# K-v products ahead of the turns of q, and three turns of x moved from TensorE to DMA, in an attention and SwiGLU kernel

One core of a Trainium2 chip. The metric is the device time of one execution in microseconds (us), the median of several. Engines: PE is TensorE, PEld its weight loads, DVE VectorE, ACT ScalarE, POOL GpSimd, SP SyncE. A number such as L513 is a line of the kernel before the change; the change shifts lines only from L680 on, so the groups named here keep their line, but for the program's closing waits: L801 before, L815 after, L808 and L818 in two of the experiments.

## The reference

Linear attention with cosine weights over 8 batches of 8 heads, 576 positions and 64 columns, then a feed-forward block over the 4608 rows that come out.

```python
def phi(x, c, s):
    r = np.maximum(x, 0.0)
    return np.concatenate([r * c, r * s], axis=-1)
q_p, k_p = phi(q, cos_w, sin_w), phi(k, cos_w, sin_w)
kv  = np.einsum('bhsf,bhsd->bhfd', k_p, v)        # the "k-v products"
z   = np.sum(k_p, axis=2)
num = np.einsum('bhsf,bhfd->bhsd', q_p, kv)       # "tile products", L444 and L399
den = np.einsum('bhsf,bhf->bhs', q_p, z)[..., None] + 1e-06
x   = (num / den)                                  # to 4608 rows of 512
g, val = x @ w_gate, x @ w_val                     # 512 to 1536, L513
out = (g * (1.0 / (1.0 + np.exp(-g))) * val) @ w_out   # L549
```

## The kernel before

The rows are worked in 36 tiles of 128. Four tiles make a group: twelve gate and value columns (`ffn_fc`), then four times twelve output products (`ffn_out`). Between these, in slots, stand the pieces of attention for the tiles to come. Two inputs of a tile need a turn (transpose): q before the tile products, x before the gate. Each is done on PE with a copy out of PSUM (`banks` in the views), or by a DMA transpose from SP. Code counts batches from 0; the text calls `b = 1` batch two, `b = 3` batch four.

```python
def relu_slots(b, lo, hi):
    ...
    relu_op("dve", st["qp"][:, b, lo:hi].rearrange("p c j (i d) -> p c (j i) d", i=2),
            raws[b, "q"][:, :, lo:hi].rearrange("p g c d -> p c g d"))

def qturn_pe(b, j, lo, hi, eng):                    # 7 turns of q and one copy out of PSUM
    ps = take(1).bitcast(BF16).rearrange("p (c x) -> p c x", x=P)
    for c in range(lo, hi):
        nc.tensor.transpose(out=ps[:, c - lo], in_=st["qp"][:, b, c, j], identity=ident)
    copy_op(eng, qt_of(b)[:, :, j, lo:hi].rearrange("p e c s -> p c e s"), ...)

def kv_mm(b): ...                                   # 72 products, L285, into two PSUM banks
def kv_out(b, engs=("act", "dve"), js=slice(0, J)): ...   # bank 0 on ACT, bank 1 on DVE, 2 copies each
...
def x_turn(t, fast=False):
    if fast:
        x_turn_pe(t)                                # four transposes on PE, L485
        x_turned(t, "act")                          # copy of 128x512
    else:
        nc.sync.dma_start_transpose(out=xT_of(t), in_=st["x", t])
...
at("b11", q_(1, 0, 0), q_(1, 1, 0), lambda: kv_mm(1), lambda: kv_out(1))
at((0, 0), lambda: kv_free(1), a_(4, 0), a_(4, 1))  # tile 4, after four output products
...
for nm in ("q", "k", "v"):                          # load_behind: one after the other
    load(b, nm)
...
elif tg == 2:                                       # tiles 9, 10, 11
    at((10, 11, 12)[i - 1] + SLOTS, lambda t=t: a_tile2(t))
    at((12, 13, 14)[i - 1] + SLOTS, turn(t, True))
```

## Time and profile before

| | us |
|---|---|
| median of three runs (lowest, highest) | 325.91 (325.68, 326.50) |
| span of the profiled run | 324.0 |
| PE busy | 317.4 |
| PE's waits, four in all | 2.7 |

The prediction below shows the page, PE's waits and the chain around both places that the change touches. ScalarE and VectorE at the first place (timeline, kernel before; columns: start us, us, engine, line, operation, output and input, then in brackets the idle time before it and its releaser):

```profile
38.74 1.08 DVE L220 TENSOR_SCALAR r_q<-raw_q 128x1792 bf16<-128x1792 bf16 x1
...
40.47 1.71 ACT L333 COPY phit<-banks 128x896 bf16<-128x896 bf16 x2 [1.66 <-PE banks L274]
42.10 0.76 ACT L297 CAST kvd<-banks 64x260 bf16<-64x260 f32 x2
42.15 0.87 DVE L297 CAST kvd<-banks 64x260 bf16<-64x260 f32 x2 [1.07 <-PE banks L285]
```

The one ReLU of 1.08 us stands between PE and its next work. The k-v copies (L297) end at 43.02, just as PE, with four output products done in the meantime, comes to the tile products that read them.

Second, SP's own waits at the end of the program (waits of SP; waited for: us in total, times, longest). It closes by waiting for the last transfers of the result:

```profile
SPq L801 <- DMA out_dram<-ob: 1.3, 2, 0.8
```

### The profile page before, as it was taken

Reading aid. Unit: us, or ns where it says so; the run is one execution under the profiler, and the core shown is the slowest. Engines: PE = TensorE matmul, PEld = TensorE weight load, DVE = VectorE, ACT = ScalarE, POOL = GpSimd, SP = SyncE. Lnnn points to the kernel's source line nnn. Section 1 sums busy time; section 2 is a strip of 40 time slices with the busy share of each in tenths; the row PEclk is TensorE's granted clock in tenths of the full one; section 3 lists DMA queues with packets and bytes.
Section 4 is the critical chain, followed back from the end, with each engine's and each line's share of the span. In section 5 each row is a group of like instructions: output and inputs, shape, how many; then the busy total and the mean of one; then the engine's idle time right before and its main releaser. Section 6 shows DMA issues by size and latency. Waiting matters only on the chain.

```text
span 324.0 us, 6046 instructions
## 1 busy us (share of the span) xinstructions
PE 317.4 (98%) x2396; PEld 159.8 (49%) x2396; DVE 181.5 (56%) x362; ACT 132.2 (41%) x242; POOL 34.9 (11%) x59
## 2 busy tenths in 40 slices
PE   8899899999999999999999999999999999999995
PEld 4596455455445444544454445444554445444443
DVE  7873867786475647565657555755564236423420
ACT  7453455653553335332632354344432132213311
POOL 6845002002000200020002000200000000000000
PEclk9999999999999999999999999999999999999999
DMA  7999998999675997699778969697921411240014
GB/s 274 211 200 197 206 190 119 219 119 156 146 121 80 162 184 122 91 140 145 172 106 114 172 149 129 87 170 158 135 45 35 104 26 34 40 104 19 0 32 99
DMA packets 72748, 40.64 MB, mean 125 GB/s; under 512 B 48272, under 2 KB 67472, under 8 KB 72720
## 3 DMA queue, kind: packets, MB, share of 16 engines
q1 hardware_dynamic: 50368, 22.55, 38.3%
q0 software_dynamic: 22192, 17.57, 37.4%
q8 instruction: 19, 0.31, 0.4%
q10 hardware_dynamic: 160, 0.13, 0.1%
q14 instruction: 9, 0.07, 0.1%
HBM read 37.75 MB, written 9.44 MB: 146 GB/s over the span
## 4 chain that ended last, share of the span: by engine, by line
PE 93%; DVE 4%; ACT 1%; issue 0%; ACTq 0%
PE banks L513 57%; PE banks L549 28%; PE banks L285 3%; PE banks L399 2%; DVE v L239 1%; PE banks L444 1%; PE banks L381 1%; PE banks L485 1%; DVE raw_k L220 1%; PE banks L568 1%; DVE ht L524 0%; DVE qwT L369 0%; PE banks L274 0%; ACT L184 0%; DVE r_q L220 0%
## 5 line engine op out<-in xcount | busy, mean ns | idle before, releaser
L524 DVE TENSOR_TENSOR ht<-sg,banks 128x512 bf16<-128x512 bf16 (+2 forms) x116 | 74.7, 649 | 69.6 <-PE banks L513 63.1
L519 ACT ACTIVATE sg<-banks 128x512 bf16<-128x512 f32 (+2 forms) x116 | 65.8, 568 | 112.7 <-PE banks L513 109.7
L513 PE MATMUL banks<-xT,wv_sb 128*128 128x512 bf16 (+2 forms) x464 | 111.3, 364 | 0.0
L513 PE MATMUL banks<-xT,wg_sb 128*128 128x512 bf16 (+2 forms) x464 | 111.3, 364 | 0.0
L549 PE MATMUL banks<-wo_sb,ht 128*128 128x512 bf16 x420 | 94.3, 379 | 0.0
L513 PEld LDWEIGHTS <-wv_sb 128*128 128x128 bf16 x464 | 44.9, 98 | 48.7
L513 PEld LDWEIGHTS <-wg_sb 128*128 128x128 bf16 x464 | 43.3, 98 | 43.2
L549 PEld LDWEIGHTS <-ht 128*128 128x128 bf16 x420 | 40.2, 98 | 45.1 <-issue 0.2
L556 ACT COPY ob<-banks 128x512 f32<-128x512 f32 x18 | 10.5, 585 | 50.9 <-PE banks L549 48.9
L235 DVE TENSOR_TENSOR r_q<-raw_q,tab 128x1152 bf16<-128x1152 bf16 x24 | 17.9, 754 | 20.2 <-ACT raw_q L218 20.2
L556 DVE COPY ob<-banks 128x512 f32<-128x512 f32 x17 | 11.7, 691 | 28.3 <-PE banks L549 27.4
L239 DVE TENSOR_TENSOR v<-raw_v,tab 128x1152 bf16<-128x1152 bf16 x31 | 23.0, 752 | 0.2 <-ACT raw_v L580 0.2
L421 DVE TENSOR_TENSOR x<-banks,rec 128x512 bf16<-128x512 f32 (+1 forms) x32 | 21.6, 674 | 1.3 <-PE banks L381 0.3
L218 ACT ACTIVATE raw_k<-raw_k 128x576 bf16<-128x576 bf16 (+1 forms) x25 | 17.3, 695 | 0.0
L730 POOL COPY hold<-phit 1x2 bf16<-1x2 bf16 x5 | 0.9, 175 | 141.2 <-DMA phit<-r_q 141.2
L218 ACT ACTIVATE raw_q<-raw_q 128x576 bf16<-128x576 bf16 x24 | 15.7, 680 | 0.9 <-DMA raw_q<-in_q_dram 0.8
L399 PEld LDWEIGHTS <-phit 128*128 128x128 bf16 (+1 forms) x240 | 9.9, 100 | 6.0 <-issue 1.3
L399 PE MATMUL banks<-kv,phit 128*128 128x65 bf16 (+1 forms) x240 | 11.5, 195 | 0.0
L152 PE MATMUL banks<-zeros 128*128 128x64 bf16 (+1 forms) x64 | 9.4, 310 | 1.0 <-DVE zeros L147 1.0
L308 DVE CAST kv<-banks 64x260 bf16<-64x260 f32 x12 | 5.1, 428 | 7.4 <-ACT kv L308 7.3
L285 PEld LDWEIGHTS <-raw_k 64*64 64x64 bf16 x504 | 7.5, 106 | 2.6 <-issue 2.5
L285 PE MATMUL banks<-v,raw_k 64*64 64x130 bf16 x504 | 8.7, 218 | 0.0
(81 smaller groups left out, 134.1 us busy)
## 6 DMA issues: line engine op xcount, KB each, us to landing
out_dram<-ob SPq DMA_DIRECT2D x70, 128.0 KB, 2.4
raw_k<-in_k_dram POOLq DMA_DIRECT2D x7, 576.0 KB, 10.8
raw_q<-in_q_dram POOLq DMA_DIRECT2D x6, 576.0 KB, 7.3
raw_v<-in_v_dram POOLq DMA_DIRECT2D x6, 576.0 KB, 13.2
wo_sb<-in_moe_w_out_dram POOLq DMA_DIRECT2D x3, 512.0 KB, 12.8
wg_sb<-in_moe_w_gate_dram POOLq DMA_DIRECT2D x5, 256.0 KB, 9.8
wv_sb<-in_moe_w_val_dram POOLq DMA_DIRECT2D x5, 256.0 KB, 10.0
wo_sb<-in_v_dram SPq DMA_DIRECT2D x2, 576.0 KB, 4.1
```

Of the source, the lines that this page charges most:

```text
L152: nc.tensor.matmul(out=ps, lhsT=zeros, rhs=zeros[:, 0:cols].unsqueeze(1).to_broadcast([P, 4, cols]), start=True, stop=True)
L218: nc.scalar.activation(out=out, in_=in_, func=AF.Relu)
L235: nc.vector.tensor_tensor(out=st[b, "q"][:, g], in0=o.unsqueeze(2).to_broadcast([P, NC, 2, D]), in1=tab, op=ALU.mult)
L239: nc.vector.tensor_tensor(out=v2s[b % 2][:, g, :, :, 0:D], in0=(first if b == 0 and g == 0 else {"v": raw_of(b, "v")})["v"][:, g].unsqueez ...
L285: nc.tensor.matmul(out=ps[i * D:(i + 1) * D, e, j * 2 * D1:(j + 1) * 2 * D1], lhsT=raws[b, "k"][es, g, c], rhs=v2s[b % 2][es, g, c, :, 0:D ...
L399: nc.tensor.matmul(out=ps[ms, e, g * D1:(g + 1) * D1], lhsT=phit[b][:, e, g, c:c + n].rearrange("p c s -> p (c s)"), rhs=kv2s[b % 2][:, e, ...
L421: nc.vector.tensor_tensor(out=st["x", t].rearrange("p (y e d) -> p e y d", e=2, d=D)[:, :, ys], in0=ps[:, :, 0:2 * J * D1].rearrange("p e ...
L513: nc.tensor.matmul(out=st["f", tg, fc, lo][i], lhsT=(wg_sb, wv_sb)[i][:, kc, fs], rhs=xT[tg][:, ts, kc], start=(kc == 0), stop=(kc == KC - 1))
L519: nc.scalar.activation(out=sg[:, 0:n], in_=st["f", tg, fc, lo][0], func=AF.Silu)
L524: nc.vector.tensor_tensor(out=hts[tg % 2][:, fc, r:r + n], in0=st.pop(("s", tg, fc, lo))[:, 0:n], in1=ps[1], op=ALU.mult)
L549: nc.tensor.matmul(out=o_ps[t], lhsT=hts[tg % 2][:, fc, r:r + P], rhs=wo_sb[:, fc], start=(fc == 0), stop=(fc == FC - 1))
L556: (nc.scalar.copy if t % 2 == 0 else nc.vector.tensor_copy)(out=ob, in_=ps)
```

## The change

Part one: the k-v products go ahead of the turns of q, so that PE need not wait for the ReLU of q; that ReLU is split over ACT and DVE, and one of the two copies of turned q goes to DVE. Part two: x of tiles 9 to 11 is turned by DMA and not by PE; to have the DMA queues free, k and v of batch four are loaded only behind the turn of tile 10, and what reads them comes later. (The slot of batch five's loads moves too, `b < 5` for `b == 3`. The diff is cut at the dots.)

```diff
-        if g == 2:
-            at(s, lambda: relu_slots(1, 0, CUT))
-    at("b11", q_(1, 0, 0), q_(1, 1, 0), lambda: kv_mm(1), lambda: kv_out(1))
+    at("b10", lambda: relu_slots(1, 0, CUT, slice(0, 1), "act"), lambda: relu_slots(1, 0, CUT, slice(1, 2)))
+    at("b11", lambda: kv_mm(1), q_(1, 0, 0), q_(1, 1, 0, "dve"), lambda: kv_out(1))
...
-        for nm in ("q", "k", "v"):
+        load(b, "q")
+        if b > 3:
+            load_kv(b)
...
+    def load_3():
+        nc.gpsimd.tensor_copy(out=hold2, in_=xT[2][0:1, 2, 0, 0:2])     # waits for the turn of tile 10
+        load_kv(3)
...
-            at(p0 + 3 if b == 3 else p0 + 1, lambda b=b: load_behind(b))
-        tk = (s0 + 4, s0 + 8 if b == 2 else s0 + 5)
+            if b == 3:
+                fs, tq = [p0 + 12 + i for i in range(4)] + [s0 + 4, s0 + 4, s0 + 5, s0 + 5], (s0 + 2, s0 + 2)
+            at(p0 + 3 if b < 5 else p0 + 1, lambda b=b: load_behind(b))
+        tk = (s0 + 4, s0 + {2: 8, 3: 7}.get(b, 5))
...
-            at((10, 11, 12)[i - 1] + SLOTS, lambda t=t: a_tile2(t))
-            at((12, 13, 14)[i - 1] + SLOTS, turn(t, True))
+            at((9, 10, 11)[i - 1] + SLOTS, lambda t=t: a_tile2(t), turn(t))
+            if i == 2:
+                at(11 + SLOTS, load_3)
         else:
+            if t in (13, 14, 15):
+                s = SLOTS * 2 + t - 4
```

More of the change, by code (lines that the diff above doesn't have):

```diff
@@ L261, in qturn_dma, with relu_slots @@
         )
-    def relu_slots(b, lo, hi):
+    def relu_slots(b, lo, hi, js=slice(0, J), eng="dve"):
         if "qp" not in st:
@@ L267, in relu_slots @@
             st["qp"] = both.rearrange("p (b c j x) -> p b c j x", b=2, c=NC, j=J)
-        relu_op("dve", st["qp"][:, b, lo:hi].rearrange("p c j (i d) -> p c (j i) d", i=2),
-                raws[b, "q"][:, :, lo:hi].rearrange("p g c d -> p c g d"))
+        relu_op(eng, st["qp"][:, b, lo:hi, js].rearrange("p c j (i d) -> p c (j i) d", i=2),
+                raws[b, "q"][:, 2 * js.start:2 * js.stop, lo:hi].rearrange("p g c d -> p c g d"))
     def qturn_pe(b, j, lo, hi, eng):
@@ L730, in load_behind, with load_kv @@
         nc.gpsimd.tensor_copy(out=hold2, in_=phit[b - 1][0:1, :, 0, 0, 0])
-        for nm in ("q", "k", "v"):
+        load(b, "q")
+        if b > 3:
+            load_kv(b)
+    def load_kv(b):
+        for nm in ("k", "v"):
             load(b, nm)
+    def load_3():
+        nc.gpsimd.tensor_copy(out=hold2, in_=xT[2][0:1, 2, 0, 0:2])
+        load_kv(3)
     for b in range(2, B):
```

## The prediction

> **What bounds the kernel now.** I read the page first (busy shares, the chain that ended last), then TensorE's (PE's) waits, then the chain and the timeline around the two places that the change touches.
>
> The page:
> ```profile
> PE 317.4 (98%) x2396; PEld 159.8 (49%) x2396; DVE 181.5 (56%) x362; ACT 132.2 (41%) x242; POOL 34.9 (11%) x59
> ...
> PE 93%; DVE 4%; ACT 1%; issue 0%; ACTq 0%
> ```
> PE is busy for 317.4 of 324.0 us and 93% of the chain is PE work at full granted clock. So nothing is to be had but work that leaves PE's queue, or the few holes in it. PE's own waits are only four, 2.7 us in all:
> ```profile
> PE banks L152 <- DVE zeros L147: 1.0, 1, 1.0
> PE banks L274 <- DVE r_q L220: 0.9, 1, 0.9
> PE banks L381 <- DVE qwT L369: 0.6, 1, 0.6
> PE banks L356 <- DVE qf L348: 0.2, 1, 0.2
> ```
> The second is the hole that the first half of the change aims at. The chain, in order of time (start, us, what):
> ```profile
> 38.15 0.67 DVE v L239
> 38.82 1.00 DVE r_q L220
> 39.83 0.05 issue
> 39.87 0.95 PE banks L274 x14
> 40.83 1.18 PE banks L285 x71
> 42.01 0.97 PE banks L549 x4
> 42.97 0.59 PE banks L444 x8
> ```
> PE's last gate and value products are issued by about 38.8 (the timeline starts the last four at 37.96, 0.216 us apart). It then waits for the ReLU of q (L220) until 39.87, turns q of batch two (14 transposes), makes the k-v products (72, L285), fills 0.97 us with output products (L549) and comes to tile 4's products (L444), which need both.
>
> The second place, the output section of the first full group, in the same view:
> ```profile
> 80.77 0.22 PE banks L485 x4
> ...
> 83.84 0.22 PE banks L485 x4
> ...
> 86.66 0.22 PE banks L485 x4
> 86.88 2.59 PE banks L549 x12
> 89.47 10.36 PE banks L513 x48
> ```
> Three times four transposes of x (tiles 9 to 11) stand in a queue without holes, 0.22 us each.
>
> **What the Trainium skill says.** (1) "VectorE: DVE Perf Modes", section "The three transpose paths", has transposes on TensorE (to PSUM) and by the DMA crossbar (to SBUF) for a full block, the DMA's the longer. The trace agrees: a tile of four blocks costs PE 0.22 us of queue, and by DMA about 1.2 us of issue and 2.4 to 10.8 us to landing, so the move pays only where nobody waits. (2) "DMA: Bandwidth & Descriptors", section "Queues, rings and completion order": each DMA engine takes turns between the queues that have work. The trace agrees: the transpose of x issued at 70.1, with no load under way, landed in 2.5 us, those issued between 105 and 112, beside three loads, in 8.6 to 9.5. That is why the change also holds back k and v. (3) The same page, section "Why PSUM operands drop a tier": an operand in PSUM allows two elements a cycle at most, and one for fp32. The trace agrees: the ReLU of turned q, 128x512 bf16 from PSUM, took 424 ns on VectorE, the float32 copy of 512 took 691 (and 260 took 428, so 1.04 ns each and 0.16 us fixed).
>
> **Part one: k-v products ahead of the turns.** Instruction order on PE: the 72 products now stand before the 14 transposes; counts are equal. On VectorE (DVE) the two last v multiplications stand together, then half the ReLU (128x7x128), then the last product of the gate, then one copy of turned q that ScalarE (ACT) did before. ACT gets the other half of the ReLU.
>
> - DVE: v of 0.67 at 38.15, second v to 39.49. PE starts the first half of the k-v products at 38.83 (36 times 16.4 ns = 0.6, to 39.42); the second half needs the second v, 39.55 with 0.05 for the semaphore, so it ends at 40.15. Nothing idle but 0.1, where before 0.9 was.
> - The ReLU halves: ACT's 896 elements at the slope of its two ReLU rows (576 in 676 ns, 1152 in 1156: 0.83 ns each) are 0.94 us. q lands at 37.7 (issued 27.1, 10.6 to landing), so ACT is done at 38.7 and the SiLU due at 38.22 is 0.4 late; its reader on DVE now runs at 40.0, so this is free. DVE's half is about 0.55 (half of 1.08), done at 40.05. Both precede 40.15.
> - Turns from 40.15 to 41.05, output products (0.86) to 41.9. Then tile 4 wants the copies: turned q on ACT from 40.75 (0.6 after the start of the turns, as before) for 0.87, then k-v on ACT 2 x 0.37: done at 42.35. On DVE turned q from 41.15; 896 elements at 0.52 ns (the 424 ns row, less 0.16 fixed, over 512) are 0.62, then k-v 2 x 0.43: done at 42.65. Tile 4's first product of the second half can start at 42.7, and the five left take 0.35: end at **43.05**.
> - Before, this end was at 43.56. So of the 0.9 us hole only **0.5 us** come through: the copies to SBUF, which waited for the k-v products before, wait for the turns now, and the wait moves from ahead of L274 to L444 (0.8 us there, of which 0.1 or 0.2 was there before).
>
> **Part two: x by DMA.** It removes 12 transposes (3 x 0.22 = **0.66 us** off PE's queue) and 3 copies of 0.58 on ACT, which is not a bound. It adds three DMA issues of 1.2 us on SyncE (SP). The products of tiles 9 to 11 come one step earlier (after gate columns 9, 10, 11), those of 13 to 15 later; their number is unchanged.
>
> - Tile 9 now follows the k-v copies of batch three directly: DVE ends these at 74.11, PE arrives at 74.10. Wait 0.05 us.
> - x of tile 9, 10, 11 is ready at about 76.1, 78.2 and 80.2 (DVE: gate product 0.69 and 0.16 + 0.20 + 0.69 of a tile, in steps of 2.0 us). SP is free until the output of 81.4. q of batch four, alone now, lands at 78.5 (72.6 + 5.9). Tile 11, issued at 80.3, lands near 83, up to 86 where k starts beside it. PE wants it at 88.8 (89.47 less 0.66). Nothing waits.
> - k and v of batch four go out at about 81 and 82, land after 8.7 to 12.7 us, so by 95. They are used from 97.4 on (five columns of 1.73 after 88.8), the k-v products come at about 103, two columns later than before. Tile 13, the first that needs them, comes at 107, tile 15 at 111.5 as before (112.47). Nothing waits.
>
> Sum: 325.91 - 0.50 - 0.66 + 0.05 = **324.8 us**.
>
> **Rivals.**
> (a) The first half gives nothing: if DVE's copy of turned q runs at one element a cycle (1.04 ns by the float32 rows: 0.157 + 0.93 = 1.09 us instead of 0.62), or it or ACT starts late, tile 4 ends at 43.5 as before. For: the copies are serial, and four are in the way. Against: the 424 ns row. Time 325.25.
> (b) The x of tile 11 becomes a new wait: were it to take 9.5 us to land as beside three loads, it would land at 89.8 and PE would idle 1.0 us ahead of L513. For: k's load starts in its landing. Against: it is issued before that load gets far, and only one of the three loads is ahead. Time 325.8.
> (c) k and v of batch four land late, ACT and DVE stop at their ReLU and multiplication, and PE runs out of banks near 100. For: they leave 8 us later than before and share the queues with eight outputs and the turns of q. Against: 2.4 us of slack even at the longest landing of such a load in this part of the trace, 12.7. Time 326 to 328.
> (d) The hole of part one closes fully: PE's own sum from 38.83 is 1.2 + 0.9 + 0.86 + 0.45 = 3.4, end 42.25, a gain of 1.3. Against: the copies above. Time 324.0.
>
> **Range and chances.** The centre is the sum. (d) is the floor, since no other work leaves PE: 324.0. (a) and (b) together give 326.2, and the three runs before spread over 0.8 us; I take 326.0 as upper end. A 2% change is 6.5 us, six times what the change can win, and a loss of it would need several such stalls as (c): faster 0.01, same 0.97, slower 0.02.
>
> **What would show it.** Right: in the profile after, PE's wait at L274 is gone, L285 starts at about 38.8 and ahead of the turns; the first L444 products begin near 41.9 but stretch to 43.0 or 43.1; DVE's 128x896 copy takes about 0.6 us; L485 has 24 transposes instead of 36; the next group's first L513 starts 1.1 us earlier, at 88.3. Every later piece keeps its length, so the lead is the same at the end. Wrong: a wait of PE at L513 near 88 on a DMA of xT (b), ACT's L218 or DVE's L239 idle on a DMA of raw_k or raw_v near 97 to 103 (c), or a lead of less than 0.2 us at 43.5 (a).

## The result, and the profile after

The changed kernel takes 325.04 us (median of 4 runs, 324.84 to 325.12) where the kernel before took 325.85 (4 runs, 325.68 to 326.50); the ratio is 0.9971, interval 0.9953 to 0.9988. A ratio here is the mean time of one kernel's fast runs over the mean of the other's in the same rounds, so it is not quite the ratio of the medians (0.9971 is 0.94 us, the medians differ by 0.81).

The page of the changed kernel:

```profile
span 323.2 us, 6031 instructions
...
PE 316.1 (98%) x2384; PEld 159.0 (49%) x2384; DVE 180.9 (56%) x363; ACT 130.7 (40%) x239; POOL 35.3 (11%) x60
```

PE has 12 instructions fewer, the turns of x. PE's waits (engine, line, waited for, us in total, times, longest):

```profile
PE banks L356 <- DVE qf L348: 1.3, 1, 1.3
...
PE banks L444 <- ACT kvd L297: 0.2, 1, 0.2
```

The 0.9 us at L274 is gone and 0.2 us at L444 has come; the two waits left out are as before. (L356 lies in the start-up, which neither part touches; it differs from run to run, 0.2 to 1.3 us or none, and its effect is mostly swallowed by the work behind it.) The chain at the first place, changed kernel (start, us, what):

```profile
38.88 1.27 PE banks L285 x69
40.15 0.51 PE banks L274 x7
...
40.69 0.91 ACT phit L333
41.59 0.27 ACT kvd L297
...
41.88 0.38 ACT kvd L297
42.26 0.04 issue
42.30 0.72 PE banks L444 x7
43.02 1.83 PE banks L549 x8
```

The way to the tile products now leads off PE, over a copy of turned q and two k-v copies on ACT; before, it led over the ReLU on DVE and then stayed on PE. Tile 4's products end at 43.02 where they ended at 43.56. The start-up gave 0.10 of it: the last value products of the first group start at 37.86, before at 37.96. From there the stretch is 5.16 us instead of 5.60, so **part one gives 0.44 us**.

VectorE at the same place (timeline, changed kernel):

```profile
39.30 0.42 DVE L220 TENSOR_SCALAR r_q<-raw_q 128x896 bf16<-128x896 bf16 x1
...
41.08 0.63 DVE L333 COPY phit<-banks 128x896 bf16<-128x896 bf16 x1 [0.77 <-PE banks L274]
41.62 0.86 DVE L297 CAST kvd<-banks 64x260 bf16<-64x260 f32 x2
```

The second place, in the chain of the changed kernel:

```profile
71.84 1.83 PE banks L513 x8
73.67 0.36 PE banks L399 x8
...
77.99 10.36 PE banks L549 x48
88.35 10.36 PE banks L513 x48
```

The 48 output products run through with no L485 between them. The products of tile 9 take 0.36 instead of 0.26 us: they wait for the k-v copies. From the end of tile 4's products to the start of group three it is 45.33 us (88.35 less 43.02) instead of 45.91 (89.47 less 43.56): **part two gives 0.58 us** here. The lead at that point is 1.12 us: 0.10 of the start-up, which differs by 0.4 us among the profiles, and 1.02 of the two parts. It is kept to the last copy out of PSUM (319.40 against 320.51). But the spans differ by 0.8 only:

```profile
SPq L815 <- DMA out_dram<-ob: 1.6, 1, 1.6
```

This is SP's wait at the end, one of 1.6 us where there were two of 1.3 in all. About 0.3 us is given back in the last four us of the program, where nothing was changed. The experiments ask for that too.

### The profile page after: what moved, and what is told of

Read it like the earlier page. It is cut to its first block, busy times and chain, and to the rows that moved or that the text cites. A ratio compares the mean times of both kernels' runs of the same rounds, so it can differ in the third digit from the quotient of the medians.

```text
span 323.2 us, 6031 instructions
## 1 busy us (share of the span) xinstructions
PE 316.1 (98%) x2384; PEld 159.0 (49%) x2384; DVE 180.9 (56%) x363; ACT 130.7 (40%) x239; POOL 35.3 (11%) x60
## 4 chain that ended last, share of the span: by engine, by line
PE 95%; ACT 2%; DVE 2%; issue 0%; ACTq 0%
PE banks L513 58%; PE banks L549 28%; PE banks L285 3%; PE banks L399 2%; PE banks L444 1%; PE banks L381 1%; DVE v L239 1%; PE banks L152 1%; PE banks L568 1%; PE banks L325 0%; PE banks L485 0%; ACT L184 0%; ACT phit L333 0%; PE banks L274 0%; ACT ob L571 0%; DVE qwT L369 0%
## 5 line engine op out<-in xcount | busy, mean ns | idle before, releaser
L152 PE MATMUL banks<-zeros 128*128 128x64 bf16 (+1 forms) x64 | 8.5, 292 | 1.0 <-DVE zeros L147 1.0
L285 PEld LDWEIGHTS <-raw_k 64*64 64x64 bf16 x504 | 7.6, 106 | 3.0 <-issue 2.1
L285 PE MATMUL banks<-v,raw_k 64*64 64x130 bf16 x504 | 8.8, 218 | 0.0
```

Source lines behind the costliest of these rows:

```text
L152: nc.tensor.matmul(out=ps, lhsT=zeros, rhs=zeros[:, 0:cols].unsqueeze(1).to_broadcast([P, 4, cols]), start=True, stop=True)
L285: nc.tensor.matmul(out=ps[i * D:(i + 1) * D, e, j * 2 * D1:(j + 1) * 2 * D1], lhsT=raws[b, "k"][es, g, c], rhs=v2s[b % 2][es, g, c, :, 0:D ...
```

## The experiments

Eleven runs were made beside those of before and after, all correct; two of them repeat a kernel. "Stretch one" is the time from the start of the last value products of group one to the end of tile 4's products (5.60 us before, 5.16 after), "stretch two" from there to the first product of group three (45.91 and 45.33). They leave out the start-up, whose spread among profiles is 0.4 us (those value products start between 37.59 and 38.01). "Tail" is the time from the last landing of the result, in the trace's landing records, to the end of SP's last instruction (good to 0.01 us). Times are medians of five runs (four of after, six of best_plus5, the four fast ones of kvout_again), with the ratio to the kernel before in the same rounds.

| kernel | time | ratio (95%) | stretch one | stretch two | tail |
|---|---|---|---|---|---|
| before | 325.7 to 325.9 | | 5.60 | 45.91 | 0.99 |
| after | 325.04 | 0.9971 (0.9953 to 0.9988) | 5.16 | 45.33 | 1.30 |
| p1_only | 325.35 | 0.9987 (0.9975 to 1.0000) | 5.17 | 45.90 | 0.97 |
| p2_only | 325.20 | 0.9982 (0.9969 to 0.9994) | 5.60 | 45.33 | 1.29 |
| kvout_first | 324.40 | 0.9956 (0.9944 to 0.9969) | 4.73 | 45.33 | 1.29 |
| no_hold | 324.95 | 0.9970 (0.9956 to 0.9983) | 5.16 | 45.33 | 1.30 |
| copies_act | 325.61 | 0.9994 (0.9981 to 1.0006) | 5.88 | 45.33 | 1.30 |
| before_plus3 | 325.97 | 1.0006 (0.9994 to 1.0018) | 5.61 | 45.91 | 1.28 |
| after_plus5 | 325.05 | 0.9977 (0.9965 to 0.9989) | 5.16 | 45.34 | 1.47 |
| best_plus5 | 324.95 | 0.9978 (0.9965 to 0.9992) | | | 1.48 |
| after_again | 324.81 | 0.9972 (0.9958 to 0.9985) | 5.16 | 45.33 | 1.30 |
| kvout_again | 324.69 | 0.9971 (0.9957 to 0.9984) | | | |
| kvout_act5 | 324.11 | 0.9951 (0.9939 to 0.9964) | 4.73 | 45.34 | 0.98 |

### Each part alone

Edit of `p1_only`: the kernel before with the changed `relu_slots` and the changed lines at b10 and b11. Edit of `p2_only`: the changed kernel with these put back.

> Part one alone (k-v products ahead of the turns of q, ReLU and copies split; x of tiles 9 to 11 still turned on PE). My theory, that the two parts add: tile 4's products (L444 x8) end at 43.0 as with the whole change, later pieces as before with the three L485 x4 left in, lead at the start of group three (89.47 before) 0.45 to 0.55, time 325.4. Rival, that part one gains nothing alone (its hole is refilled before group one starts at 55.2): lead 0 to 0.1 at 55.2 and 325.8.

> Part two alone (x of tiles 9 to 11 by DMA, k and v of batch four behind; k-v products of batch two where they were). My theory: no change up to 72, PE waits 0.1 for the k-v copies at tile 9's products, then no L485 in the outputs of group two; lead at the start of group three 0.55 to 0.6, time 325.3. Rival, that taking PE's three turns out only shows a wait hidden under them: lead under 0.2 there, time 325.7.

Both came as the theory said, once the start-up is taken out: p1_only's raw lead at group three is 0.81 us, of which 0.37 is its earlier start, p2_only's is 0.53 with a start 0.05 later. Part one alone cuts stretch one to 5.17 and leaves stretch two; part two alone does the reverse. The lines (chains: p1_only, then p2_only):

```profile
42.76 1.83 PE banks L549 x8
...
88.66 10.36 PE banks L513 x48
```

```profile
43.61 1.83 PE banks L549 x8
...
88.94 10.36 PE banks L513 x48
```

42.76 less 37.59 is 5.17; 88.94 less 43.61 is 45.33. The stretches add up to 0.43 + 0.58 = 1.01, against 1.02 in the whole change. The two are independent. (The times, 0.47 and 0.62 under the median before, carry a start-up spread of 0.4 us and don't resolve the tail.)

### What holds tile 4's products up

Edit of `copies_act`, which lengthens the suspected cost: both copies of turned q on ACT.

```diff
-    at("b11", lambda: kv_mm(1), q_(1, 0, 0), q_(1, 1, 0, "dve"), lambda: kv_out(1))
+    at("b11", lambda: kv_mm(1), q_(1, 0, 0), q_(1, 1, 0), lambda: kv_out(1))
```

> The changed kernel with both copies of turned q on ScalarE, as before the change, and the k-v products still ahead. If the series of copies after the turns sets the end of tile 4's products, ScalarE has 0.91 + 0.91 + 0.76 from 40.69: k-v copies done at 43.2, L444 ends at 43.6 to 43.9 instead of 43.02, as late as before the change or later, time 325.7 to 325.9. Rival, that the gain came from the order on PE alone: L444 ends at 43.0 to 43.2, time 325.0 to 325.1.

Edit of `kvout_first`, which takes it away: the k-v copies, which need no turn, go ahead.

```diff
+    at("b11", lambda: kv_mm(1), lambda: kv_out(1), q_(1, 0, 0), q_(1, 1, 0, "dve"))
```

> The changed kernel with the k-v copies put ahead of the copies of turned q on both engines (order k-v products, k-v copies, turns). If the wait at L444 (41.9 to 42.6) is for a series of copies that starts only after the turns, as I hold, the k-v copies now run beside the turns on PE: ACT done with turned q by 41.6 to 41.9, DVE by 42.2, tile 4's eight products end at 42.4 to 42.6 instead of 43.02, time 324.5. Rival, that L444 is slow by itself (half-width weights, changes of shape): they still take 0.7 or more from 41.9 with the first two apart, end at 43.0, time 325.0.

The chains of copies_act, then of kvout_first:

```profile
40.49 1.72 ACT phit L333 x2
42.20 0.27 ACT kvd L297
...
42.91 0.63 PE banks L444 x7
43.54 1.83 PE banks L549 x8
```

```profile
40.74 0.37 ACT kvd L297
...
41.13 0.91 ACT phit L333
...
42.09 0.63 PE banks L444 x8
42.72 1.83 PE banks L549 x8
```

With both copies on ACT, the k-v products still ahead and the hole at L274 still closed, stretch one is 5.88 us: longer than before the change (5.60). (The end at 43.54 is below the 43.6 expected only because this run's start-up was 0.2 us ahead; its time, 325.61, is below the expected 325.7 for the same reason.) With the k-v copies first it is 4.73. PE's order is the same in all three. So closing the hole at L274 makes a gain possible, and the copies decide whether any comes through: 0.72 us is lost, or 0.43 us won, by moving a copy. (No run has PE's new order without the split of the ReLU, so their shares are not shown. An estimate from the traces: the whole ReLU of 1.08 us in place of its half at 39.30 would end at 40.4, 0.3 us after PE begins the turns at 40.09.) L444 by itself is not slow: its eight products take 0.63 when all has come.

The chain shows `kvout_first` 0.43 us ahead of the change. The times agree in direction, 324.40 against 325.04 in different rounds; a repetition in the same rounds gave less:

> The changed kernel once more, unaltered, for a comparison in the same rounds as the next two: 325.0 us; from the last landing of the result to the end of the span 1.30 us as before, whichever theory of that tail holds.

> kvout_first once more, in the same rounds: 324.4 us if its 0.6 under the changed kernel is due to the order of copies (0.43 in the chain from the last gate products on), 324.7 or more if it was the spread of the start-up.

after_again ran at 324.81, and the four fast runs of kvout_again at 324.62 to 325.17, median 324.69: 0.12 us apart. By its own bound of 324.7 this stands on the edge and settles nothing for the time. I trust the stretches, which two profiles of each order give to 0.01 us (5.16 and 5.16; 4.73 and 4.73 with kvout_act5), for the cause, and take the times for the size within a few tenths only. In the same rounds kvout_act5 (below), which has this order and also the shorter tail, ran 0.70 us under after_again, where the stretch and the tail add up to 0.43 + 0.32. The fifth run of kvout_again took 1176 us; see the end of this document.

### Is the hold-back of k and v needed?

Edit of `no_hold`: load all three of batch four one behind the other again.

```diff
         load(b, "q")
-        if b > 3:
-            load_kv(b)
+        load_kv(b)
...
-            if i == 2:
-                at(11 + SLOTS, load_3)
```

> The changed kernel, but k and v of batch four go out directly behind q of batch four, as before the change, not behind the turn of tile 10. If the hold-back is what keeps the turns of x short, the landings of tiles 9 to 11 go from 2.4 to 3.8 us to 6 to 9.5 us, and tile 11 (issued at 79.6) lands at 86 to 89 where PE wants it at 88.2: between no wait and 1.0 us of wait of PE ahead of the first L513 of group three, time 325.0 to 326.0. Rival, that the hold-back has no part in the time: landings change, PE waits for nothing, 325.0.

The landings of the turns of tiles 9 and 11 in us from issue, from the transfers of no_hold in two windows (75.6 to 76.6 us and 79.6 to 80.6 us hold the issues of the turns of tile 9 and 11):

```profile
xT<-x SPq DMA_TRANSPOSE x1, 8.7
...
xT<-x SPq DMA_TRANSPOSE x1, 6.9
```

In the changed kernel these are 3.8 and 2.4 us. Tile 11, issued at about 79.6, lands at about 86.5 instead of 82.0, and PE wants it at 88.2. The rival holds: PE has no wait there, stretch two is 45.33 and the time 324.95. The hold-back shortens the turns, as it was meant to, but the time doesn't need it; what it buys is slack, 6 us in place of 1.7. It costs nothing either: k and v of batch four land at 87.6 and 91.6 and are first read at 96.7 and 97.7.

### Where the last 0.3 us went

The program's transfers from SP and ACT take eight semaphores in turn, and at its end SP waits for all eight in a fixed order. In the trace each such wait takes about 0.06 us, passed or not. Before, the last transfer to land is the sixth of the eight; two waits are left. Part two adds three transfers on SP, and the last one to land is now the first waited for; seven are left, 5 x 0.06 = 0.3 us more. (The trace's records of SP: before, the last landing at 322.98 is met by a wait at 322.99, two more follow at 323.05 and 323.11, and SP goes on at 323.18. After, the landing at 321.85 is met at 321.87, seven waits follow up to 322.30, and SP goes on at 322.37.) Edits: small transfers of 64 bytes near 260 us, where SP is idle, three more in the kernel before (to make the order that of after) and five more in the changed one (to complete the round of eight).

```diff
+    spare = consts.tile([1, 5, 16], FP32)
+    def spare_loads():
+        for i in range(5):
+            nc.sync.dma_start(out=spare[:, i], in_=q[0, 0, i:i + 1, 0:16])
+    at(SLOTS * 7 + 2, spare_loads)
```

> The kernel before with three transfers of 64 bytes added on SyncE at about 260 us, where it is idle, so that the last transfers of the result come on the same semaphores of the round of eight as in the changed kernel. In all kernels with part two (after, p2_only, kvout_first, no_hold) the span ends 3.80 to 3.83 us after the start of the last copy, in before and p1_only 3.49 and 3.50. If the place in the round sets the order of SyncE's closing waits and so costs 0.3 us, this kernel's tail becomes 3.8 and its time 326.1. Rival, that the tail has to do with part two's transposes or its other times: tail 3.5, time 325.8.

> The changed kernel with five such transfers of 64 bytes at about 260 us, so that the last transfers come on the semaphores that they had before the change. If the place in the round costs the 0.3 us, the tail returns to 3.5 and the time is 324.7, the lead of PE in the chain staying 1.02 to 1.1. Rival: tail 3.8, time 325.0.

(These texts count the tail from the start of the last copy instead: 3.51 us in before, 3.81 in after and before_plus3, 3.99 in after_plus5.)

before_plus3 shows the tail of the changed kernel without anything else of it: 1.28 us from the last landing to the end, and in SP's waits the single 1.6:

```profile
SPq L808 <- DMA out_dram<-ob: 1.6, 1, 1.6
```

Its time, 325.97, is 0.1 (medians) or 0.2 us (means) over the kernel before in the same rounds, less than the 0.3 expected and with an interval that includes none, so it is the tail in the trace that shows the cause. after_plus5 failed: its waits are as before again (1.3 in two), the last landing is followed by two waits, but then SP's next instruction comes 0.41 us after the last of these, where it comes after 0.06 to 0.07 in the other kernels, and the tail is 1.47. The same is seen in best_plus5. In both, SP issues 125 transfers where it issues 117 or 120 in all others (the text below says "instructions"); what is late there I don't know. One more thing differs in these two alone: a packet of 8 KB of an instruction queue (q14) starts at 322.94, inside the span, where in the others none starts in the last 70 us of it. As it starts 0.6 us after the late instruction, it shows no cause. So the five transfers went to ACT, one for each of five gate columns, on top of kvout_first:

```diff
+    spare = consts.tile([1, 5, 16], FP32)
+    for i in range(5):
+        at(SLOTS * 7 + i, lambda i=i: nc.scalar.dma_start(out=spare[:, i], in_=q[0, 0, i:i + 1, 0:16]))
```

> kvout_first with the five transfers of 64 bytes issued by ScalarE, one for each of five gate columns near 260 us, so that the last transfers come on the same semaphores as before the change while SyncE has no more instructions than in the changed kernel. In after_plus5 two closing waits were left after the last landing instead of seven, as theory said, but SyncE's next instruction then came 0.41 us late, which it did in none of the kernels with 117 or 120 instructions on SyncE. Theory: from the last landing to the end of the span 0.98 to 1.0 us instead of 1.30, time 324.1. Rival, that the late instruction goes with the place in the round and not with SyncE's length: 1.4 to 1.5 us, time 324.5.

```profile
SPq L818 <- DMA out_dram<-ob: 1.3, 2, 0.7
```

The tail is 0.98 us and the time 324.11, as expected and the best of all: 0.9951 of the kernel before. The place in the round sets the tail: 0.97 to 0.99 us in before, p1_only and kvout_act5, 1.28 to 1.30 in before_plus3 and in all kernels that have part two without spare transfers.

### Tile 4 behind more output products

Edit of `best_plus5`: kvout_first with the spare transfers on SP, and tile 4 one slot later.

```diff
-    at((0, 0), lambda: kv_free(1), a_(4, 0), a_(4, 1))
+    at((0, 0), lambda: kv_free(1))
+    at((0, 1), a_(4, 0), a_(4, 1))
```

> The changed kernel with the k-v copies first (kvout_first), tile 4's eight products behind two groups of output products instead of one, so that no copy is waited for, and the five small transfers. Theory: L444 x8 take 0.45 to 0.5 instead of 0.72 and begin at once; chain 0.3 to 0.4 shorter than in kvout_first (whose group three starts 45.33 after L444's end), tail 3.5, time 323.7 to 323.9. Rival, that moving tile 4 makes its x late for group two at 54: PE waits at the first L513 there and the gain is lost, 324.2 or more.

Neither. No x came late, and the tile products no longer wait for copies (they take 0.56 us, expected 0.45 to 0.5), but PE reaches the output products before their weights (PE's waits, best_plus5):

```profile
PE banks L549 <- DMA wo_sb<-in_moe_w_out_dram: 0.3, 1, 0.3
```

The first part of the output weights is issued at 28.75 and lands 12.4 us later, at 41.15. In the changed kernel it lands at 40.42, and PE comes at 40.88. So the next bound lies 0.5 us behind in that profile, and its place varies: this load lands between 40.0 and 41.15 in the profiles of the kernels with part one, and a PE that comes to the output products earlier waits for it. after_plus5, whose start-up was 0.14 us ahead, met it too, for 0.2 us, and its stretch one came out at 5.16 all the same, as the copies were the later. The start-up spread and the late instruction at the end hide the rest; the time of best_plus5 says little.

## Why the prediction was right

The time was 325.04, predicted 324.8, in the range of 324.0 to 326.0. Its times are on the clock of the profile before; the profile after started up 0.10 us earlier, so that 0.10 is to be added to the measured times below when they are set beside predicted ones. Step by step:

- **The hole at L274 closes** (0.9 us): right. PE's waits have no L274, and L285 starts at 38.81.
- **Only 0.5 us of it comes through, as the copies now wait for the turns**: right, 0.44. The end of ACT's copies was put at 42.35 and was 42.25, of DVE's at 42.65 and was 42.48, that of tile 4's products at 43.05 and was 43.02 (so 43.12 on the old clock: the near hit is in part luck, and the gain 0.44, not 0.51). copies_act and kvout_first show the cause, not only the size.
- **DVE's copy at 0.52 ns an element, 0.62 us**: right, 0.63. Rival (a) falls with it; copies_act shows what a longer series of copies does. (The section "Why PSUM operands drop a tier", from which this was argued, stands on the page "VectorE: DVE Perf Modes"; the prediction, in the words cut from its (3), put it on the DMA page.)
- **Part two takes 0.66 us off, less a wait of 0.05**: right in kind; the wait for the k-v copies at tile 9 cost 0.1, and 0.58 was left.
- **Nothing waits for the turns or for k and v**: right. Tile 11 was put at "near 83" and landed at 82.0; rival (b), 9.5 us beside the loads, did not come even when no_hold made the turns take 8.7 us, since it was issued early enough. Rival (c): k and v landed 9.1 and 6.1 us before their first use.
- **"Every later piece keeps its length, so the lead is the same at the end"**: wrong by 0.31 us. It held up to the last copy, 1.11 us ahead of before (0.10 of it start-up), but not for the program's closing waits, whose order part two shifted. This is the step of the sum that failed: 1.11 - 0.31 = 0.80, the measured difference of the spans. The lead predicted was 1.11 too (0.50 + 0.66 - 0.05), which the two parts alone, at 1.02, did not reach; the start-up filled the rest by chance. The prediction counted transfers for their time and missed that their number sets which semaphore the last one uses.

What stays open: the 0.2 to 0.4 us of start-up spread between executions, and why SP's instruction is late in after_plus5 and best_plus5.

## What to carry to other kernels

When a wait ahead of a busy engine is taken away, follow the consumers of both operations that were exchanged: the wait often moves to the first reader of the later one, and what comes through is set by the copies between them. So order the copies by what they need, not by where they stood: a copy that needs no turn goes ahead of one that does. For gains of under 1 us, look at the ends too: a transfer more or less can change the order in which the program's last waits are met.

## What the Trainium skill lacked or had wrong

- "VectorE: DVE Perf Modes", section "The three transpose paths": 390 ns on TensorE and 1309 ns by DMA for a block of 128x128. In this stream four blocks on PE cost 0.22 us of queue together (0.055 each, though each product is 0.22 from start to end), and a DMA turn of four blocks landed 2.4 to 2.5 us after issue alone, 3.8 us beside the end of one load, and 6.9 to 8.7 us beside k and v as well. The section has neither the cost in a full queue nor that beside other transfers, and these decided between the paths here.
- "DMA: Bandwidth & Descriptors", section "Queues, rings and completion order": has the turn-taking, which the landings fit, but nothing on closing waits. No page has that the end of a program waits for its transfer semaphores one after the other at 0.06 us each, here up to 0.31 us by where the last transfer stands in the round.
- "TensorE: Matmul & The Clock Gate", part 1: has a gate at half of the clock, and warns that the clock's trace events are unreliable on trn2 and that the gate has been seen stuck at a quarter for 50 us and more. One execution of kvout_again, which took 1176.48 us, may be of that kind, but lasted from end to end: 48 gate and value products that take 10.36 us elsewhere took 39.38, 3.8 times as long, and a product from start to end 1031 to 1058 ns against 364, while VectorE and ScalarE kept their times (651 and 568 ns for their largest groups, against 648 and 568 in kvout_first) and the granted clock was recorded as 1.000. The page gives no such slowing for a whole execution, and I have no cause for it; it was seen once in all these executions and is left out of every comparison.
